# Gated linear attention into an activation-gated MLP: state decays taken by transfers through memory instead of by products on TensorE

## The chip, the cores and the metric

The kernel runs on one core of a Trainium2 chip. The metric is the device time of one execution in microseconds. TensorE (PE) multiplies matrices into PSUM, VectorE (DVE), ScalarE (ACT) and GpSimd (POOL) work elementwise, and SyncE (SP) issues most of the transfers between memory and the on-chip buffers. Each engine, and each issuing queue, takes its instructions in the order in which they stand in the program.

## What is computed

The first part is a recurrence per batch and head, over 768 steps with a head size of 48 (4 batches, 8 heads). The state is a 48 x 48 matrix; each of its rows decays by its own factor `alpha` at each step:

```python
for t in range(S):
    state = alpha[:, :, t, :, None] * state + np.einsum('bhd,bhe->bhde', k[:, :, t], v[:, :, t])
    y[:, :, t] = np.einsum('bhd,bhde->bhe', q[:, :, t], state)
```

The second part takes y as 3072 tokens of 384 numbers:

```python
h = x @ w_in            # 384 -> 2048
g = h * np.cos(h)
return (g @ w_out).astype(np.float32)   # 2048 -> 384
```

## The kernel before, in words

**Tiling.** The 768 steps of a batch are cut into 3 pairs of chunks; a pair has 256 steps, a chunk 128. With 4 batches there are 12 pairs, numbered J = 0 to 11. The pairs 0, 3, 6 and 9 begin a batch with an empty state. On chip, partition p of a pair holds the steps 2p and 2p + 1 (the index e), so that partitions 0 to 63 are the first chunk and 64 to 127 the second. The 8 heads are handled as 4 head pairs (`NP`), two heads of 48 numbers in 64 rows each.

**Decays.** Within a chunk the recurrence becomes matrix products, once q and k are scaled by the decay accumulated since the chunk began. `ln` takes the logarithm of alpha (for J >= 3 GpSimd first multiplies the two steps of a partition, `mul_a`, so that one sum is enough). `cums` adds the logarithms up with a triangular matrix on TensorE (lines 158 to 169). Its result has 384 columns, one per head and component, and a row per partition. Behind them, in 8 more columns, the same function puts four products (line 167), one per head pair: the logarithms' totals over each of the two chunks, but with the components lying along the partitions. `exps` takes the exponential of all this on ScalarE; for e = 1 it reads 392 columns (line 196).

**State.** The state of a head pair has its components along the partitions, so the factor by which a chunk makes it decay is wanted along the partitions too. `decay` (line 242) forms on GpSimd a small tile `c2_sb[J]` of 128 x (4 head pairs, 2 chunks, 2 heads) from the 8 columns, with zeros where row and head don't belong together (`dmask`). `outer` makes the products of k and v of a chunk, `add_state` adds the old state on VectorE, and `decay_state` (line 310) multiplies the sum by `c2_sb` on GpSimd, which gives the state that the next chunk's y reads.

**Other steps of a pair.** `scale_k` and `scale_q` (GpSimd or VectorE) multiply k and q by the exponentials; `trans` transposes them on TensorE; `scores` and `mask` give the part within a chunk; `castv` brings v to 16 bits on GpSimd; `stack_v` (line 221) restacks it by four SP transfers from on-chip to on-chip for J >= 3; `yT` makes y, transposed, from state, scores and stacked v. Then `mlp1`, the cosine, `gate` and `mlp2` run the second part, and `store` writes the result.

**Order.** A table written out by hand, `PLAN` (lines 433 to 498), has a row for each step and a column for each pair, with a planned time in nanoseconds; the steps are issued in the order of these times. The times set the order only. An instruction starts when its engine gets to it and its inputs are there. On SP stand the loads of alpha, k, q and v (48), the stacking transfers (36) and the stores. The pools give alpha 4 buffers and k, q and v 3 each.

```python
"load v": "3750 8250 35770 41770 51910 61570 67906 73970 75470 85710 95267 96757",
"eb": "- - - 43138 49360 59320 71283 83790 88947 103219 109067 127741",
"castv": "10660 16184 42680 48680 62906 71716 73380 94337 92617 104995 130491 144063",
"vst": "- - - 49610 63836 82270 79970 98527 102027 109974 131421 151922",
"trans": "14073 17773 40885 47348 58944 70064 80866 92234 109989 116249 127239 136001",
"state 0": "14460 23600 46802 51395 70936 89767 87087 104215 121237 120457 143283 156049",
"yT": "20503 26545 48000 58219 72693 91349 90719 109104 124433 140168 151138 162701",
```

The row `eb` is a pair's run of exponentials on ScalarE, the last of which (e = 1) has the values that the state's decay is made from.

Of the kernel before, what the change touches and what calls it, by code (L numbers as in the profile page):

```python
# [9 lines left out]
FP = mybir.dt.float32  # L10
# [6 lines left out]
def kernel(  # L17
# [10 lines left out]
    nc = tc.nc  # L28
    B, H, S, D = q.shape
    DM, DF = moe_w_in.shape  # L30
    C = 128
    HC = C // 2
    T2 = 2 * C
    NJB = S // T2
    NJ = B * NJB
    NP = H // 2
    HD = H * D
    KT = DM // C
    NF = DF // C
# [1 line left out]
    NU = NF // FW  # L41
    MP = 4

    NL, NQ, NV, NS = 4, 3, 3, 2
    BUF = {"a": 4, "in": 3, "cp": 3, "qkT": 3, "A": 2, "un": 4, "us": 2, "c": 3, "xT": 3, "g": 4}

    consts = ctx.enter_context(tc.tile_pool(name="consts", bufs=1))
    sb = ctx.enter_context(tc.tile_pool(name="sb", bufs=2))
    ps = ctx.enter_context(tc.tile_pool(name="ps", bufs=1, space=bass.MemoryType.PSUM))

    zeros = consts.tile([C, 512], BF, tag="zeros")
    nc.vector.memset(zeros, 0.0)  # L52
# [11 lines left out]
    for c in range(2):  # L64
        r = slice(HC * c, HC * c + HC)
# [14 lines left out]
    for lst, nm, n in ((lna_t, "lna", NL), (kh_t, "kh", NQ), (qh_t, "qh", NQ), (vp_t, "vp", NV)):  # L80
        for r in range(n):
            t = consts.tile([C, 2, H, 64], BF, tag=f"{nm}{r}", name=f"{nm}{r}")
            nc.vector.memset(t[:, :, :, D:64], 0.0)
            lst.append(t)
    for r in range(NS):
        t = consts.tile([C, 2, H, 64], BF, tag=f"vs{r}", name=f"vs{r}")
        nc.gpsimd.memset(t[:, :, :, D:64], 0.0)
        vs_t.append(t)
    dmask = consts.tile([C, 2], FP, tag="dmask")
    nc.vector.memset(dmask, 0.0)  # L90
    for a in range(2):
# [5 lines left out]
    a_sb, kqv, cp_sb, icp_sb, qkT_sb, A_sb, c2_sb = {}, {}, {}, {}, {}, {}, {}  # L97
# [36 lines left out]
    def act_set(which):  # L134
        if which == "exp" and act_now[0] != "exp":
            nc.scalar.preload_act_table_set("natural_log_exp_and_others")  # L136
        act_now[0] = which
# [14 lines left out]
    def sums(J, t, mats):  # L152
        o = t[:, 0:HD].rearrange("p (h d) -> p h d", h=H)
        for i, m in enumerate(mats):
            nc.tensor.matmul(o, m.rearrange("p c i -> p (c i)"), lna_t[J % NL][:, i, :, 0:D], start=(i == 0),
                             stop=(i == len(mats) - 1))

    def cums(J):
        if (J, 1) not in cums_ps:
            cums_ps[J, 1] = ps.tile([C, 512], FP, tag="x", name="cums", bufs=1)  # L160
        t = cums_ps[J, 1]
        lna = lna_t[J % NL]
        ne = 1 if J in both else 2
        sums(J, t, [tri, tri][:ne])
        for p in range(NP):
            for e in range(ne):
                nc.tensor.matmul(t[:, HD + 2 * p : HD + 2 * p + 2],
                                 lna[:, e, 2 * p : 2 * p + 2, :].rearrange("s h d -> s (h d)"), inchunk,
                                 start=(e == 0), stop=(e == ne - 1))
# [10 lines left out]
    def sub(J):  # L180
        cp_sb[J, 0] = sb.tile([C, HD], FP, tag="cp0", name="cp", bufs=BUF["cp"])
        nc.vector.tensor_tensor(out=cp_sb[J, 0].rearrange("p (h d) -> p h d", h=H),
                                in0=cums_ps[J, 1][:, 0:HD].rearrange("p (h d) -> p h d", h=H),
                                in1=lna_t[J % NL][:, 1, :, 0:D], op=ALU.subtract)

    def logs(J, e):
        return cums_ps[J, e] if (J, e) in cums_ps else cp_sb[J, e]

    def icp(J, e):
        act_set("exp")  # L190
        icp_sb[J, e] = sb.tile([C, HD], FP, tag=f"icp{e}", name="icp", bufs=BUF["cp"])
        nc.scalar.activation(out=icp_sb[J, e], in_=logs(J, e)[:, 0:HD], func=AF.Exp, scale=-1.0)  # L192

    def exps(J, e):
        act_set("exp")
        w = HD + 2 * NP * e
        t = logs(J, e)
        if (J, e) not in cp_sb:
            cp_sb[J, e] = sb.tile([C, w], FP, tag=f"cp{e}", name="cp", bufs=BUF["cp"])
        nc.scalar.activation(out=cp_sb[J, e], in_=t[:, 0:w], func=AF.Exp)  # L200

    def session(J):
        for e in range(2):
            icp(J, e)
        for e in range(2):
            exps(J, e)
        if J + 1 < NJ:
            ln(J + 1)
# [29 lines left out]
    def evict_vs(J, copy):  # L238
        copy(out=vs_t[J % NS][:, :, :, 0:D],
             in_=vs_ps.pop(J)[:, :, 0:HD].rearrange("s c (h d) -> s c h d", h=H))  # L240

    def decay(J):
        c2_sb[J] = sb.tile([C, NP, 2, 2], FP, tag="c2", name="c2", bufs=4)
        nc.gpsimd.tensor_tensor(
            out=c2_sb[J],
            in0=cp_sb[J, 1][:, HD : HD + 2 * NP].rearrange("r (p c) -> r p c", c=2).unsqueeze(3).to_broadcast([C, NP, 2, 2]),
            in1=dmask.unsqueeze(1).unsqueeze(1).to_broadcast([C, NP, 2, 2]),
            op=ALU.mult,
        )
# [3 lines left out]
    def trans(J):  # L253
        T_ps[J] = ps.tile([C, 2, 2 * NP, 2, HC], BF, tag="h", name="T_ps", bufs=3)
        for i, x in ((1, kh_t[J % NQ]), (0, qh_t[J % NQ])):
            for p in range(NP):
                for e in range(2):
                    for c in range(2):
                        r = slice(HC * c, HC * c + HC)
                        nc.tensor.transpose(T_ps[J][:, c, i * NP + p, e, :],  # L260
                                            x[r, e, 2 * p : 2 * p + 2, :].rearrange("s h d -> s (h d)"), ident_bf[r, r])

    def evict_T(J, c, copy):
        if J not in qkT_sb:
            qkT_sb[J] = sb.tile([C, 2, 2 * NP, C], BF, tag="qkT", name="qkT", bufs=BUF["qkT"])
        copy(out=qkT_sb[J][:, c], in_=T_ps[J][:, c].rearrange("r n e s -> r n (e s)"))  # L266
# [145 lines left out]
    def idle(n):  # L412
# [5 lines left out]
    copies = {"DVE": nc.vector.tensor_copy, "ACT": nc.scalar.copy}  # L418
    mults = {"DVE": nc.vector, "POOL": nc.gpsimd}
    steps = {  # L420
        "load": lambda J, nm: load(nm, J), "w1": load_w1, "w2": load_w2,
        "mula": mul_a, "ln": ln, "cums0": cums0, "cums": cums, "sub": sub, "icp": icp, "exps": exps, "eb": session,
        "sk": lambda J, e, eng="POOL": scale_k(J, e, mults[eng]), "sq": lambda J, e, eng="POOL": scale_q(J, e, mults[eng]),
        "castv": cast_v, "vst": stack_v, "vpe": stack_v_pe,
        "vev": lambda J, eng="DVE": evict_vs(J, copies[eng]), "decay": decay, "trans": trans,
        "evT": lambda J, c, eng="DVE": evict_T(J, c, copies[eng]), "scores": scores, "mask": mask, "outer": outer,
        "add": add_state, "state": decay_state, "yT": yT, "evy": lambda J, c, eng="ACT": evict_y(J, c, copies[eng]),
        "m1": mlp1, "sin": cosine, "gate": gate, "m2": mlp2, "evo": lambda J, c, eng="ACT": evict_o(J, c, copies[eng]),
# [73 lines left out]
    for key, line in PLAN.items():  # L502
        kind, *rest = key.split()
        for J, word in enumerate(line.split()):
            if word != "-":
                t, _, eng = word.partition(":")
# [38 lines left out]
```

## Time and profile before

| | us |
|---|---|
| median of 3 runs | 188.01 (187.84 to 188.37) |
| profiled execution | 188.32 |
| its span, first to last instruction | 186.5 |
| TensorE busy | 176.7 (95%) |
| VectorE busy | 135.4 (73%) |
| ScalarE busy | 126.5 (68%) |
| GpSimd busy | 77.1 (41%) |

A busy share is an average over the span. The weights and the first pairs fill the first 40 us or so; from then on pairs overlap, one in its attention part while earlier ones are in the MLP. Times in the profile's rows count from the start of the span. A row of a group or of the timeline gives its start, its length, the engine, the line of the kernel, what it writes and reads, and how often it occurs; in square brackets stands the idle time before it and what ended that. `SPq` is SP's issuing queue; the length of a row there is the time that the issue held the queue, not the transfer.

### The profile page before, as it was taken

The page shows a single profiled execution, that of the slowest core. Times are in us where ns is not written, and L with a number is a line of the kernel's source. Part 1 is how long each engine was busy: PE and PEld are TensorE (multiplying, and loading weights), DVE is VectorE, ACT ScalarE, POOL GpSimd, SP SyncE. Part 2 cuts the span into 40 slices and gives each one's busy share as a digit, 9 for nine tenths or more (in the row PEclk, how much of TensorE's full clock was granted, in tenths as well). Part 3 has the DMA queues.
Part 4 walks back from the last instruction along what each step waited for, and adds up shares of the span by engine and source line. Part 5 has one row for each costly group of instructions (what it writes and reads, how often), then busy time and mean ns, then how long its engine had stood idle before and what let it go on. Part 6 is the DMA issues. An engine that isn't in the chain of part 4 may idle for free.

```text
span 186.5 us, 5746 instructions
## 1 busy us (share of the span) xinstructions
PE 176.7 (95%) x2467; PEld 126.4 (68%) x2469; DVE 135.4 (73%) x184; ACT 126.5 (68%) x161; POOL 77.1 (41%) x110
## 2 busy tenths in 40 slices
PE   7988799989989999999999999999999999999993
PEld 2434588655667786785688668676867686786872
DVE  7178775589799979698847987794977556754461
ACT  2466876889498986889668999728965264373330
POOL 5079510257645653781896076930360320100000
PEclk9999999999999999999999999999999999999999
DMA  6999999999949979996799932600041005301102
GB/s 152 261 258 165 181 204 237 259 266 265 274 105 304 264 180 245 264 260 167 186 278 278 247 104 46 182 0 4 4 136 47 5 0 158 118 0 66 64 0 84
DMA packets 60137, 29.47 MB, mean 158 GB/s; under 512 B 51024, under 2 KB 60112, under 8 KB 60112
## 3 DMA queue, kind: packets, MB, share of 16 engines
q1 hardware_dynamic: 56256, 25.86, 57.2%
q0 software_dynamic: 3712, 3.15, 11.0%
q8 instruction: 19, 0.31, 0.7%
q10 hardware_dynamic: 144, 0.10, 0.2%
q14 instruction: 6, 0.05, 0.1%
HBM read 25.17 MB, written 4.72 MB: 160 GB/s over the span
## 4 chain that ended last, share of the span: by engine, by line
PE 73%; ACT 15%; DVE 8%; issue 3%; DVEq 0%
PE h_ps L361 31%; PE o_ps L390 24%; PE idle_ps L416 4%; PE y_ps L340 3%; ACT qkT L266 3%; DVE gsb L372 3%; PE T_ps L260 2%; ACT c_sb L367 2%; PE A_ps L274 2%; ACT L136 2%; ACT cp L200 2%; PE U_ps L291 2%; DVE kh L212 2%; ACT icp L192 2%; PE o_last L384 1%
## 5 line engine op out<-in xcount | busy, mean ns | idle before, releaser
L372 DVE TENSOR_TENSOR gsb<-h_ps,c_sb 128x1024 bf16<-128x1024 f32 x48 | 58.1, 1221 | 21.9 <-ACT c_sb L367 21.2
L367 ACT ACTIVATE c_sb<-h_ps,halfpi 128x1024 bf16<-128x1024 f32 x48 | 53.0, 1113 | 26.8 <-PE h_ps L361 23.0
L361 PE MATMUL h_ps<-xT,w 128*128 128x256 bf16 x576 | 66.7, 273 | 1.3 <-ACT xT L351 0.7
L390 PE MATMUL o_ps<-w,gsb 128*128 128x384 bf16 x368 | 66.7, 327 | 0.1
L361 PEld LDWEIGHTS <-w 128*128 128x128 bf16 x576 | 55.6, 98 | 10.1 <-issue 1.6
L390 PEld LDWEIGHTS <-gsb 128*128 128x128 bf16 x368 | 33.8, 98 | 21.2 <-DVE gsb L372 0.6
L313 POOL TENSOR_TENSOR un<-us,c 128x384 bf16<-128x384 f32 x20 | 16.7, 835 | 40.7 <-DVE us L305 29.1
L279 DVE TENSOR_TENSOR A_sb<-A_ps,msk 128x1024 bf16<-128x1024 f32 x24 | 28.9, 1215 | 1.7 <-PE A_ps L274 1.7
L212 POOL TENSOR_TENSOR kh<-k,icp 128x384 bf16<-128x384 f32 x17 | 16.9, 999 | 9.2 <-ACT icp L192 7.8
L216 POOL TENSOR_TENSOR qh<-q,cp 128x384 bf16<-128x384 f32 x15 | 15.0, 1006 | 11.8 <-ACT cp L200 11.8
L149 POOL TENSOR_TENSOR a<-a 128x384 f32<-128x384 f32 x9 | 9.0, 1001 | 12.6 <-DMA a<-in_alpha_dram 12.6
L219 POOL CAST vp<-v 128x768 bf16<-128x768 f32 x12 | 10.1, 841 | 8.8 <-DMA v<-in_v_dram 7.7
L416 PE MATMUL idle_ps<-zeros 128*128 128x512 bf16 x38 | 12.0, 457 | 1.4 <-DVE zeros L52 1.2
L141 ACT ACTIVATE lna<-a 128x768 bf16<-128x768 f32 x12 | 10.2, 847 | 4.6 <-DMA a<-in_alpha_dram 4.6
L266 ACT COPY qkT<-T_ps 128x1024 bf16<-128x1024 bf16 x8 | 8.0, 1015 | 6.9 <-PE T_ps L260 4.4
L136 ACT ACT_TABLE_LOAD x9 | 11.5, 1283 | 0.9 <-PEq L529 0.7
L367 ACT ACT_TABLE_LOAD x9 | 11.5, 1283 | 0.2
L266 DVE COPY qkT<-T_ps 128x1024 bf16<-128x1024 bf16 x16 | 10.8, 678 | 1.1 <-ACT qkT L266 1.1
L305 DVE TENSOR_TENSOR us<-U_ps,un 128x384 f32<-128x384 f32 x16 | 8.7, 550 | 3.8 <-PE U_ps L291 2.8
L402 DVE COPY o_sb<-o_ps 128x384 f32<-128x384 f32 x12 | 6.6, 551 | 6.5 <-PE o_ps L390 6.5
L351 ACT CAST xT<-y_ps 128x384 bf16<-128x384 f32 x12 | 6.7, 594 | 5.6 <-PE y_ps L340 3.8
L351 DVE CAST xT<-y_ps 128x384 bf16<-128x384 f32 x12 | 6.8, 584 | 4.7 <-PE y_ps L340 2.9
(69 smaller groups left out, 159.1 us busy)
## 6 DMA issues: line engine op xcount, KB each, us to landing
k<-in_k_dram SPq DMA_DIRECT2D x12, 384.0 KB, 6.0
a<-in_alpha_dram SPq DMA_DIRECT2D x12, 384.0 KB, 6.1
v<-in_v_dram SPq DMA_DIRECT2D x12, 384.0 KB, 6.0
q<-in_q_dram SPq DMA_DIRECT2D x12, 384.0 KB, 6.3
out_dram<-o_sb SPq DMA_DIRECT2D x23, 192.0 KB, 2.6
vs<-vp SPq DMA_DIRECT2D x36, 64.0 KB, 2.1
w<-in_moe_w_out_dram POOLq DMA_DIRECT2D x4, 384.0 KB, 10.1
w<-in_moe_w_in_dram POOLq DMA_DIRECT2D x4, 384.0 KB, 7.3
```

Source lines behind the costliest of these rows:

```text
L136: nc.scalar.preload_act_table_set("natural_log_exp_and_others")
L212: eng.tensor_tensor(out=kh_t[J % NQ][:, e, :, 0:D], in0=kqv["k", J][:, :, e], in1=icp_, op=ALU.mult)
L216: eng.tensor_tensor(out=qh_t[J % NQ][:, e, :, 0:D], in0=kqv["q", J][:, :, e], in1=cp, op=ALU.mult)
L266: copy(out=qkT_sb[J][:, c], in_=T_ps[J][:, c].rearrange("r n e s -> r n (e s)"))
L279: nc.vector.tensor_tensor(out=A_sb[J][:, c].rearrange("s a p t -> s (a p) t"), in0=A_ps.pop((J, c)).rearrange("s a p t -> s (a p) t"), in1 ...
L313: nc.gpsimd.tensor_tensor(out=u, in0=U_sum.pop(n), in1=c2_sb[J][:, :, c].unsqueeze(3).to_broadcast([C, NP, 2, D]), op=ALU.mult)
L351: copy(out=xT[J][:, :, c * C : (c + 1) * C].rearrange("r i (t e) -> r i e t", e=2), in_=y_ps[J][:, c, 0 : KT * C].rearrange("r (i e t) -> ...
L361: nc.tensor.matmul(h_ps[J, u][:, f, :], w1[:, kk, ft * C : (ft + 1) * C], xT[J][:, kk, :], start=(kk == 0), stop=(kk == KT - 1))
L367: nc.scalar.activation(out=c_sb[J, u], in_=h_ps[J, u], func=AF.Sin, bias=halfpi, scale=1.0)
L372: nc.vector.tensor_tensor(out=gsb[J][:, u * FW : (u + 1) * FW], in0=h_ps.pop((J, u)), in1=c_sb.pop((J, u)), op=ALU.mult)
L390: nc.tensor.matmul(o_ps[J, c][:, 0:DM], gsb[J][:, ft, c * C : (c + 1) * C], w2[:, ft], start=(ft == 0), stop=(ft == NF - 1))
L416: nc.tensor.matmul(idle_ps[0], zeros[:, 0:C], zeros, start=True, stop=True)
```

## The change

For the pairs 3 to 11 (`NE = 3`) the four products of `cums` are left out, and the exponential for e = 1 reads 384 columns instead of 392. The totals over a chunk are the last rows of the cumulative sums, so their exponentials stand already in the rows 63 and 127 of `cp_sb[J, 1]`. A new step `ends` writes these two rows (2 x 384 numbers of 4 bytes) to a scratch tile in memory, `[4, 2, 2, 48]`. `decay` then reads them back by two transfers, one for each head of the head pairs, into 48 partitions each, number by number, so that the components lie along the partitions. The target is one of four tiles `dec_t`, zeroed once by GpSimd at the start. All three transfers are issued by SP. GpSimd's multiply by `dmask` is gone for these pairs. The new step comes 2.3 us behind the planned start of the exponentials in `PLAN`, the reads 3.6 us behind `ends`.

```diff
+    NE = 3
...
-    NL, NQ, NV, NS = 4, 3, 3, 2
+    NL, NQ, NV, NS, ND = 4, 3, 3, 2, 4
...
+    dram = ctx.enter_context(tc.tile_pool(name="dram", bufs=1, space=bass.MemoryType.DRAM))
...
+    dec_t = []
+    for x in range(ND):
+        t = consts.tile([C, NP, 2, 2], FP, tag=f"dec{x}", name=f"dec{x}")
+        nc.gpsimd.memset(t, 0.0)
+        dec_t.append(t)
...
-        for p in range(NP):
+        for p in range(NP if J < NE else 0):
...
-        w = HD + 2 * NP * e
+        w = HD + (2 * NP * e if J < NE else 0)
...
+    ends_dram = {}
+
+    def ends(J):
+
+        ends_dram[J] = dram.tile([NP, 2, 2, D], FP, tag="ends", name="ends", bufs=3)
+        nc.sync.dma_start(out=ends_dram[J].rearrange("p c a d -> c p (a d)"),
+                          in_=cp_sb[J, 1][HC - 1 : C : HC, 0:HD].rearrange("c (p x) -> c p x", p=NP))
+
     def decay(J):
+        if J >= NE:
+            c2_sb[J] = dec_t[J % ND]
+            rows = ends_dram.pop(J)
+            for a in range(2):
+                nc.sync.dma_start(out=c2_sb[J][64 * a : 64 * a + D, :, :, a].rearrange("r p c -> r (p c)"),
+                                  in_=rows[:, :, a].rearrange("p c d -> d (p c)"))
+            return
...
-        "decay": "11579 11749 45180 49450 56180 80800 76050 92447 114345 115465 132991 146818",
+        "decay": "11579 11749 45180 49038 55260 65220 77183 89690 94847 109119 114967 133641",
+        "ends": "- - - 45438 51660 61620 73583 86090 91247 105519 111367 130041",
```

In the changed program SP's order around the places that the prediction names is: store, `ends` 3, load k 4, store, load q 4, the reads for pair 3, stacking of pair 3, `ends` 4, load v 4, load k 5, store, load a 7, the reads for pair 4, five loads (the last of them v 5), `ends` 5, stacking of pair 4, the reads for pair 5, store, load a 8, load v 6. TensorE's, VectorE's and ScalarE's other instructions keep their order.

More of the change, by code (lines that the diff above doesn't have):

```diff
@@ L424 @@
         "castv": cast_v, "vst": stack_v, "vpe": stack_v_pe,
-        "vev": lambda J, eng="DVE": evict_vs(J, copies[eng]), "decay": decay, "trans": trans,
+        "vev": lambda J, eng="DVE": evict_vs(J, copies[eng]), "ends": ends, "decay": decay, "trans": trans,
         "evT": lambda J, c, eng="DVE": evict_T(J, c, copies[eng]), "scores": scores, "mask": mask, "outer": outer,
```

## The prediction

> **What bounds the kernel now.** I read the page's busy shares first, then the windows by stage, then the timelines of TensorE, SP's queue and GpSimd around the places that the change touches. The page:
>
> ```profile
> span 186.5 us, 5746 instructions
> PE 176.7 (95%) x2467; PEld 126.4 (68%) x2469; DVE 135.4 (73%) x184; ACT 126.5 (68%) x161; POOL 77.1 (41%) x110
> PEclk9999999999999999999999999999999999999999
> q1 hardware_dynamic: 56256, 25.86, 57.2%
> out_dram<-o_sb SPq DMA_DIRECT2D x23, 192.0 KB, 2.6
> v<-in_v_dram SPq DMA_DIRECT2D x12, 384.0 KB, 6.0
> ```
>
> TensorE is busy nearly throughout, at full clock. GpSimd (POOL) has room. A load takes 6.0 us to land although a store on a quiet queue takes 1.9 (the shortest waits in SP's rows): SP's transfers stand in a line. The windows say where (columns: stretch, its length, then PE, PEld, DVE, ACT, POOL busy with counts, clock, DMA share, GB/s):
>
> ```profile
> 51.29:55.96 4.67, 4.08 (x56) 3.25 (x51) 4.54 (x7) 4.64 (x8) 2.24 (x3) 1.00 0.47 106
> 55.96:69.95 13.99, 13.97 (x187) 10.71 (x186) 12.69 (x16) 12.57 (x15) 8.03 (x10) 1.00 1.08 249
> 69.95:83.94 13.99, 13.73 (x237) 10.13 (x236) 11.38 (x15) 10.69 (x14) 9.29 (x12) 1.00 1.12 256
> 93.27:107.26 13.99, 13.87 (x251) 11.06 (x249) 10.31 (x12) 11.25 (x14) 7.80 (x10) 1.00 1.09 268
> 107.26:135.00 27.74, 27.44 (x439) 20.36 (x437) 22.01 (x29) 22.09 (x30) 14.54 (x18) 1.00 0.21 57
> ```
>
> From 56 to 84 us both TensorE and the DMA engines are full, so work added to SP's line comes out as later landings of everything behind it. After 107 us the DMA engines are a fifth busy. The change adds to the line in the first kind of stretch.
>
> **What it removes.** Nine pairs (the fourth to the twelfth) lose four products each on TensorE. One pair's cumulative sum and products:
>
> ```profile
> 54.48 0.33 PE L155 MATMUL cums<-lna,tri 128*128 128x384 bf16 x1
> 54.65 0.24 PE L167 MATMUL cums<-inchunk,lna 128*128 128x2 bf16 x4
> 54.76 1.49 PE L361 MATMUL h_ps<-xT,w 128*128 128x256 bf16 x12
> ```
>
> The record of 0.24 us is pipelined; from the first product's start to the next matmul's is 54.76 - 54.65 = 0.11 us. Nine times 0.11 is 1.0 us. The chain that ended last gives each group 0.08 us, so 0.7 us is the other bound; I take 0.9. GpSimd loses nine multiplies of 0.217 us (row of L244); it is off the path but for one place below. The exponential of the second half loses 8 of 392 columns: its 0.487 us against 0.471 for the same without them, 9 x 0.016 = 0.1 us on ScalarE, counted as nothing because ScalarE's idle time in front of it (1 to 4 us in most pairs) covers it. The four memsets of the new tiles (0.10 us each by the row of a small memset) fall into GpSimd's 7.3 us of idle time before its first cast.
>
> **What it adds to SP.** Per pair three issues: `ends` (8 pieces of 384 bytes to memory), then two reads of 384 pieces of 4 bytes each, 768 packets. Bounds of each price:
> - An issue: 0.33 us (shortest store) to 0.60 (the stacking transfers, 0.587 median). I take 0.5, as most of SP's issues here come close behind each other.
> - A 4-byte packet: 9 ns is the median of the 4-byte semaphore packets in the trace's packet records; the mean over the queue's packets is 57.2% x 186.5 x 16 / 56256 = 30 ns. No row has 4-byte data. Over 16 engines a pair's 48 packets per engine take 0.43 to 1.44 us; I take 0.45, since the records of 384, 1024 and 1536 bytes (25, 46 at the least, 62 ns) lie near a line that ends near 10 ns at no bytes.
> - `ends` to land: 1.9 us on a quiet queue, 6.1 at most for a store in the crowd; I take 4 to 5 where loads stand ahead of it.
>
> The Trainium skill, "DMA: Bandwidth & Descriptors", section "Rules for kernel authors", says that a last dimension that isn't contiguous is lowered to one descriptor per element; the count of 768 agrees with it, and no run here shows it yet. The same page's section "Bandwidth" gives about 10.5 ns per packet in its smallest transfer; an estimate by that is 48 x 10.5 = 0.50 us a pair, beside my 0.45.
>
> **Where it lands on the path.** SP issues in order, and the read of a pair waits until its own `ends` has landed; what stands behind waits too. SP's line before:
>
> ```profile
> 48.13 0.43 SPq L105 DMA_DIRECT2D q<-in_q_dram  x1
> 50.86 3.01 SPq L225 DMA_DIRECT2D vs<-vp  x4
> 62.92 2.38 SPq L105 DMA_DIRECT2D v<-in_v_dram  x1
> 65.93 3.50 SPq L225 DMA_DIRECT2D vs<-vp  x4
> 69.47 0.58 SPq L408 DMA_DIRECT2D out_dram<-o_sb  x1
> 70.10 0.46 SPq L105 DMA_DIRECT2D a<-in_alpha_dram  x1
> 70.61 0.68 SPq L105 DMA_DIRECT2D v<-in_v_dram  x1
> ```
>
> The last row is the v of pair 6 (pairs from 0). It landed at 75.61 us, and GpSimd, in order, was standing there for it:
>
> ```profile
> 75.76 0.83 POOL L219 CAST vp<-v 128x768 bf16<-128x768 f32 x1 [1.09 <-PE y_ps L340]
> 81.33 1.00 POOL L216 TENSOR_TENSOR qh<-q,cp 128x384 bf16<-128x384 f32 x1
> 83.34 0.41 PE L260 MATMUL T_ps<-ident_bf,kh 64*128 64x64 bf16 x16
> ```
>
> (The page names a matmul as releaser; the landing came 0.1 us before it.) From the cast to 83.45 GpSimd has no gap, and the product at 81.33 to 82.32 feeds the transposes at 83.34: a slack of 1.0 us, 1.2 once the multiply at 78.45 is gone.
>
> How late is that v? Ahead of it stand three pairs' nine new issues. Pair 3's fit into SP's gap of 2.3 us before 50.86, less its read's wait, and overshoot it; with `ends` of pair 4 that is 0.7 us at 56. Pair 4's reads are issued while loads hold SP back (1.4 to 2.4 us an issue), so that only their 0.45 us of packets count, and I let the ring's own stalls absorb that. Pair 5's `ends` goes out behind the v load of 62.92, which landed at 69.96, so it lands near 70.5, 1.0 us after the stacking transfers leave SP free; its two reads then cost 2 x 0.5 = 1.0 of issue and 0.4 of packets ahead of the v. Sum 0.7 + 1.0 + 1.0 + 0.4 = 3.1 us. TensorE stalls 3.1 - 1.2 = 1.9 us at the transposes. At the low prices (0.33, 9 ns, `ends` landed in time) the sum is 0.4 + 0 + 0.7 + 0.4 = 1.5, a stall of 0.3; at the high ones (0.60, 30 ns, 2.0 of wait) 0.9 + 2.0 + 1.2 + 1.4 = 5.5, a stall of 4.3.
>
> Other places. Pair 3's decay was used at 53.72; I put its landing at 53.4 to 54.2 (ends out at 46.5, landed near 50, reads out by 51, 2 to 3 us to land behind a k, a store and a q). VectorE's next use of that state came 1.0 us after it was ready, so 0.1 us counted, 0.7 at most. From pair 4 on the decay was used 10 us or more after it can land (73.07, 90.2, 92.9, 107.4). The stacked v of pairs 5 and 7 had 3.6 and 4.3 us before their y products at 94.4 and 112.4; the line will be 3 to 5 us late there, but TensorE itself is then 1.9 late, so nothing counted. After 107 us SP waits long for other things (11.4 us before 135.36), which hides pairs 9 to 11; stores that land late there cost nothing until a copy needs their buffer (0.95 us once before).
>
> Sum: -0.9 + 1.9 + 0.1 = +1.1 us. The profiled execution took 188.32 us (span 186.54), 0.31 above the median of 188.01; so 189.4 beside it, and 189.1 as a median.
>
> **Rivals.** A, faster: the line has more give than I count, because a load held back by a full ring absorbs SP's issues; then the v is under 1.2 us late and only the gain is left, 188.0 - 0.9 = 187.1. It decides at a lateness of 2.1 us (stall equal to gain). For it: SP's issue times of 1.4 to 2.4 us in 56 to 65 are waits, not work. Against: rows of 0.46 to 0.68 around the v, where SP was the limit. B, slower by much: a 4-byte packet costs 50 ns or more. Then a pair takes 2.4 us of every engine, the v of pair 6 is near 6 late (stall 4.6), and six pairs push the stacked v of pair 7 some 12 us, past its 4.3 and the stall: 188.0 + 4.6 + 3 = 195. Nothing in the rows speaks for 50 ns, but none shows a read of 4 bytes either. The Trainium skill, same page, "Specifications", says that transfers under 512 bytes are done as read and write-back; by that rule a packet would cost twice, 60 ns at the upper row, which is this rival. The 384-byte loads at 25 ns a packet show no such doubling. C: the two halves cancel, with a lateness between 1.5 and 2.7: 187.5 to 188.5.
>
> **Chances.** Mine (slower by 0.6 to 3 us) 0.43, A 0.25, B 0.19, C 0.13. Below 0.3% (0.56 us) this kernel's runs, 187.84 to 188.37, tell little from no change. Faster 0.26, same 0.14, slower 0.60. The likeliest case alone spans 188.6 to 191; the range takes in A's 187.1 and the lower part of B, 187.0 to 194.5.
>
> **What would show it.** Right: products of L167 fall from 60 to 24; SP's waits name the `ends` landing at the reads; GpSimd's cast of v of pair 6 stands about 3 us later, and TensorE is idle 1 to 3 us before that pair's transposes; GpSimd never waits long for a decay after pair 3. Wrong: no TensorE gap there (A), or DMA share above 1 well past 107 us and y products waiting for stacked v (B).

## The result and the profile after

The changed kernel takes 189.18 us (median; 188.80 to 189.62) where the kernel before, run beside it, takes 188.31 (187.84 to 188.40). The ratio is 1.0052 with an interval of 1.0034 to 1.0070: slower by 0.98 us by that ratio. The forecast was 1.1 us. The profiled execution that is read below took 189.34 us, span 187.6; the one of before 188.32, span 186.5. One execution further down, of the repeated change, showed a lower granted clock (0.989, 193.09 us) and is left out of every median and ratio.

The lines of the page of the changed kernel that answer to those of before:

```profile
span 187.6 us, 5704 instructions
PE 175.7 (94%) x2431; PEld 124.7 (66%) x2433; DVE 136.1 (73%) x184; ACT 126.7 (68%) x161; POOL 75.6 (40%) x105
...
q1 hardware_dynamic: 63546, 25.92, 59.2%
...
PE 58%; DMA 13%; ACT 9%; DVE 6%; SPq 5%; POOL 4%; issue 3%; POOLq 0%; ACTq 0%; DVEq 0%
```

TensorE has 36 matmuls less and is busy 1.0 us less, at the same clock, but its span is 1.1 us longer: it stands 2.1 us more. The last line shows where to look. It is the share of each engine in the chain that ended last; before the change it read 73% TensorE, 15% ScalarE, 8% VectorE and no transfer at all. Now 18% of the chain is transfers and SP's queue.

The reads themselves, by source line (duration of an issue in ns, least, median and most; then us from issue to landing in the same order):

```profile
L264 SPq DMA_DIRECT2D dec<-ends x18: 327/525/1137, 49.1 to 139.6; - x18
DMA to landing us min/median/max: 2.0/3.4/3.7
L256 SPq DMA_DIRECT2D ends<-cp x9: 539/553/1197, 46.8 to 133.7; - x9
```

They are cheap: half a us per issue. The view gives a landing for only four of the 18 reads, so 3.7 us is not the longest: pair 3's second read is issued at 50.15 us and lands at 54.44. And in the packet records of this trace the 7,200 or so packets that are new are 9 ns each (median of all that are 4 bytes long, 9,091 records). What they cost is order. This is the chain around pair 6's v (start, length, what):

```profile
66.06 3.69 DMA ends<-cp
69.76 0.97 SPq L264
...
72.28 4.95 DMA v<-in_v_dram
...
82.83 0.97 POOL qh L225
```

Pair 5's `ends` takes 3.69 us to land; SP waits for it at the head of the reads, 0.4 us beyond the stacking transfers; then the reads, a store and a load of alpha (`a`) go, and the v of pair 6 is issued at 72.28 instead of 70.61 and lands at 77.24 instead of 75.61. GpSimd casts it 1.6 us later, works without a gap up to the q product of pair 6, and TensorE's transposes of q wait for that. The changed kernel, and behind it the transposes of q before:

```profile
77.38 0.83 POOL L228 CAST vp<-v 128x768 bf16<-128x768 f32 x1 [2.62 <-DMA v<-in_v_dram]
...
83.30 0.41 PE L284 MATMUL T_ps<-ident_bf,kh 64*128 64x64 bf16 x16
83.85 0.41 PE L284 MATMUL T_ps<-ident_bf,qh 64*128 64x64 bf16 x16
```

```profile
83.58 0.40 PE L260 MATMUL T_ps<-ident_bf,qh 64*128 64x64 bf16 x16
```

Before, the second group of transposes followed the first (at 83.34) after 0.24 us, now after 0.55: a stall of 0.31 us, where the forecast had 1.9. It is in the right place and far too small. The rest comes from two places that the forecast had costed at nothing. The first is the y product of pair 7, whose stacked v landed 5.3 us later than before (113.46 against 108.12); the second is a store, which holds the buffer that ScalarE's next copy needs. After, and then the same product and copy before:

```profile
113.38 0.79 PE L364 MATMUL y_ps<-A_sb,vs 128*32 128x128 bf16 x32 [0.53 <-DMA vs<-vp]
...
142.24 0.48 ACT L426 COPY o_sb<-o_ps 128x384 f32<-128x384 f32 x1 [2.95 <-DMA out_dram<-o_sb]
142.77 2.11 PE L414 MATMUL o_ps<-w,gsb 128*128 128x384 bf16 x12 [0.47 <-ACT o_sb L426]
```

```profile
112.79 0.62 PE L340 MATMUL y_ps<-A_sb,vs 128*32 128x128 bf16 x32
140.03 0.48 ACT L402 COPY o_sb<-o_ps 128x384 f32<-128x384 f32 x1 [0.95 <-DMA out_dram<-o_sb]
```

The store stands behind the stacking of pair 10, which held SP 3.33 us instead of 2.39, and behind pair 11's reads, 1.07 us more. (Only the reads are known to be the change's doing; the longer hold occurs without any transfer too, as told below under late stores.) It goes out at 140.17 us instead of 137.85 and lands at 142.14 instead of 139.95. ScalarE waits 2.95 us for it (0.95 before), and TensorE's output matmuls wait for ScalarE.

How late TensorE is against before, from the starts of the same groups of matmuls in the two timelines (negative: ahead; gains of the left-out products are included):

| stretch, us | late by, us | what happened |
|---|---|---|
| to 60 | -0.06 | pair 3's reads, no stall |
| 63 to 67 | +0.34 | a product of VectorE took 1.16 us instead of 0.55; made good by 78 us |
| 83, before pair 6's transposes | -0.03 | |
| behind them | +0.28 | v of pair 6 |
| 106 to 112 | -0.13 | products left out |
| behind pair 7's y | +0.76 | stacked v of pair 7 |
| behind pair 9's transposes | +0.18 | a wait that was there before is gone |
| 131 to 141 | +0.21 | |
| 144.7 to the end | +1.26 | store |

So in this execution the last place decides: 1.05 of the 1.26 us come at the store.

### The profile page after: what moved, and what is told of

Read it like the earlier page. It is cut to its first block, busy times and chain, and to the rows that moved or that the text cites. A ratio compares the mean times of both kernels' runs of the same rounds, so it can differ in the third digit from the quotient of the medians.

```text
span 187.6 us, 5704 instructions
## 1 busy us (share of the span) xinstructions
PE 175.7 (94%) x2431; PEld 124.7 (66%) x2433; DVE 136.1 (73%) x184; ACT 126.7 (68%) x161; POOL 75.6 (40%) x105
## 3 DMA queue, kind: packets, MB, share of 16 engines
q1 hardware_dynamic: 63546, 25.92, 59.2%
## 4 chain that ended last, share of the span: by engine, by line
PE 58%; DMA 13%; ACT 9%; DVE 6%; SPq 5%; POOL 4%; issue 3%; POOLq 0%; ACTq 0%; DVEq 0%
PE h_ps L385 24%; PE o_ps L414 21%; DMA a<-in_alpha_dram 6%; PE y_ps L364 3%; ACT qkT L290 3%; DMA v<-in_v_dram 3%; DVE gsb L396 2%; ACT c_sb L391 2%; PE A_ps L298 2%; DMA ends<-cp 2%; PE T_ps L284 2%; PE U_ps L315 2%; SPq L234 2%; DMA vs<-vp 2%; DVE kh L221 2%
## 5 line engine op out<-in xcount | busy, mean ns | idle before, releaser
L337 POOL TENSOR_TENSOR un<-us,dec 128x384 bf16<-128x384 f32 x15 | 12.5, 835 | 40.3 <-DVE us L329 25.9
L440 PE MATMUL idle_ps<-zeros 128*128 128x512 bf16 x38 | 11.1, 428 | 1.4 <-DVE zeros L55 1.2
L426 ACT COPY o_sb<-o_ps 128x384 f32<-128x384 f32 x11 | 5.2, 477 | 8.2 <-PE o_ps L414 5.1
```

The lines of the kernel that those rows point to most:

```text
L337: nc.gpsimd.tensor_tensor(out=u, in0=U_sum.pop(n), in1=c2_sb[J][:, :, c].unsqueeze(3).to_broadcast([C, NP, 2, D]), op=ALU.mult)
L426: copy(out=t, in_=o_ps.pop((J, c))[:, 0:DM])
L440: nc.tensor.matmul(idle_ps[0], zeros[:, 0:C], zeros, start=True, stop=True)
```

## The experiments

The theory is that the price is lateness on SP's one queue: three issues a pair and the read's wait for its own `ends` push back loads, stackings and stores that have no slack. Its rivals: the left-out products themselves bring nothing or even cost; the number of small packets costs, wherever they stand; one single place (pair 3's late decay, pair 6's v, the store) makes the whole loss.

**The gain alone.** The products stay out, and nothing is transferred. This kernel leaves out the states that are carried from chunk to chunk in pairs 3 to 11, and serves for timing only.

```diff
         if J >= NE:
             c2_sb[J] = dec_t[J % ND]
-            rows = ends_dram.pop(J)
-            for a in range(2):
-                nc.sync.dma_start(...)
             return
...
-        "ends": "- - - 45438 51660 61620 73583 86090 91247 105519 111367 130041",
```

> The products are left out as in the change, but none of the transfers is made: the decays of pairs 3 to 11 are the zeros that the four tiles were filled with, so these states are left out of the result in effect. It measures the gain alone. Both theories: 36 products at 25 ns, of which the traces before and after show 0.8 us freed between matmuls: 0.6 to 0.9 us below the kernel before, ratio 0.995 to 0.997. If the gain is only there as long as nothing else limits, under 0.3 us.

Measured: 187.87 us against 188.40, ratio 0.9974 (0.9962 to 0.9986): a gain of 0.5 us (0.3 to 0.7), which lies between the two expectations. In its trace TensorE is ahead by 0.6 us from 110 us on.

**The cost alone.** Products and GpSimd's multiply stay for all pairs; the transfers are made and nobody reads the tiles.

```diff
-        for p in range(NP if J < NE else 0):
+        for p in range(NP):
...
+    def reads(J):
+        rows = ends_dram.pop(J)
+        for a in range(2):
+            nc.sync.dma_start(out=dec_t[J % ND][64 * a : 64 * a + D, :, :, a]..., in_=rows[:, :, a]...)
...
+        "reads": "- - - 49038 55260 65220 77183 89690 94847 109119 114967 133641",
```

> All products and GpSimd's multiplies stay as before; the 27 transfers are made as in the change, to tiles that nothing reads. It measures the cost alone. If gain and cost simply add, the cost is what the change lost plus the gain: 0.9 + 0.8 = 1.7 us above the kernel before (1.3 to 2.1). If waiting for the decay itself costs (a state that stands for its transfer), this is well under 1.3, because nothing waits for these tiles.

Measured: 189.71 us, ratio 1.0071 (1.0044 to 1.0098): a cost of 1.3 us (0.8 to 1.8). Cost and gain add up to 0.8, which fits the change's 0.98 within the intervals. The products do bring something, so the first rival is out; the loss lies in the transfers. In this kernel's profile pair 6's transposes are held 1.0 us and pair 7's y 0.9 us.

**Half of the pairs each.** The change for the pairs 3 to 8 alone, and for 9 to 11 alone; the others keep the products and the decay of before.

```diff
-    NE = 3
+    NE, N2 = 3, 9      # or 9, 12
...
-        if J >= NE:
+        if NE <= J < N2:
```

> The change for pairs 3 to 8 only; pairs 9 to 11 as before. Theory V (as predicted): the loss comes from the crowded stretch of 46 to 107 us, through v of pair 6 and the stacked v of pair 7; then this kernel is 0.7 us or more above the kernel before, all of the change's loss or more. Theory S: the loss that lasts is made at 140 us, where ScalarE's copy stands for a store that pair 11's transfers delayed; then this kernel is within 0.5 us of the kernel before, and TensorE is 0 to 0.3 us late at 140 us.

> The change for pairs 9 to 11 only. Theory V: nothing is crowded there, the three pairs' gain of 0.25 us is left: 0 to 0.3 below the kernel before. Theory S: ScalarE waits 2 us or more for a store near 140 us and the kernel is 0.5 to 1.0 us above the kernel before.

Measured: pairs 3 to 8 188.98 us, ratio 1.0031 (1.0008 to 1.0054), +0.6 us; pairs 9 to 11 188.63 us, ratio 1.0016 (0.9996 to 1.0035), +0.3 us with an interval that takes in nothing. Together +0.9, the change's own loss. Each value lies between what the two theories had named. By the medians neither half makes it all, though the first half's interval (0.2 to 1.0 us) reaches the change's 0.98, so this pair of runs alone doesn't settle it. The profile of the second half has a hold of TensorE of 0.90 us at 99.3 us, ahead of every changed pair and named by nothing that the profile shows, and the store's wait of 2.1 us then costs only 0.17; so it does not settle what the store is worth.

The profile of the first half shows the one thing that the forecast had as a bound: pair 3's reads landed at 56.23 us, and GpSimd, VectorE and TensorE stood in a row behind them (its timeline):

```profile
56.38 0.83 POOL L337 TENSOR_TENSOR un<-us,dec 128x384 bf16<-128x384 f32 x1 [5.71 <-DMA dec<-ends]
57.25 0.56 DVE L329 TENSOR_TENSOR us<-U_ps,un 128x384 f32<-128x384 f32 x1 [1.78 <-POOL un L337]
57.87 2.36 PE L385 MATMUL h_ps<-xT,w 128*128 128x256 bf16 x20 [1.78 <-DVE us L329]
```

In the changed kernel's profile, whose program is the same up to there, these reads landed at 54.44 and TensorE did not stand there. So pair 3 has next to no slack, and a landing that varies by 1.8 us decides whether it costs.

**Pair 3 left as before, and then the same transfers put elsewhere.** The first kernel has the change for the pairs 4 to 11 only. The second issues just as many transfers of the same kind, but pair 5's and pair 8's stand behind the loads and stackings that they were ahead of, and pair 11's reads behind the stores:

```diff
-    NE = 3
+    NE, N2 = 4, 12
...
-        "decay": "11579 11749 45180 49450 55260 65220 77183 89690 94847 109119 114967 133641",
-        "ends": "- - - - 51660 61620 73583 86090 91247 105519 111367 130041",
+        "decay": "11579 11749 45180 49450 55260 76000 77183 89690 105000 109119 114967 137000",
+        "ends": "- - - - 51660 68000 73583 86090 102500 105519 111367 130041",
```

> The change for pairs 4 to 11; pair 3 keeps its products. In the profiles pair 3's reads landed at 54.4 in one execution and at 56.2 in another, where VectorE can wait until about 54.7. If that is a cause of the loss, the times lie closer together than the change's and the median comes 0.1 to 0.8 us below it (one pair's gain of 0.1 us is given up, and three issues ahead of v of pair 6 are gone). If it is not, the same as the change or 0.1 above.

> Pair 3 keeps its products; the transfers of pair 5 stand behind v of pair 6, those of pair 8 behind the stacking transfers of pair 8, the reads of pair 11 behind three stores. Only the place of transfers on SP's queue changes. If the loss is made of the four places (pair 3's late decay, v of pair 6, the stacked v of pair 7, the store at 140 us), all four are eased and the gain is what is left: 0.2 to 0.5 us below the kernel before, 187.9 to 188.2. If the transfers cost in another way (contention for the engines, longer issues everywhere), it stays at 188.8 or more.

Measured on one chip: 190.79 us, ratio 1.0136 (1.0100 to 1.0173), and 188.09 us, ratio 0.9994 (0.9973 to 1.0016). The same 24 transfers, with the same packets, cost 2.7 us more or less by their place in the queue. The first kernel misses what was expected of it: without pair 3 it is, on this chip, no closer to the kernel before. This takes out the number of packets as a cause, and pair 3 as the only one. The kernel with the early places, its waits (engine and line, what it waited for, us in total, times, longest) and pair 6's transposes in its timeline:

```profile
ACT o_sb L426 <- DMA out_dram<-o_sb: 3.0, 1, 3.0
PE T_ps L284 <- POOL qh L225: 1.2, 1, 1.2
PE y_ps L364 <- DMA vs<-vp: 1.1, 1, 1.1
```

```profile
83.23 0.41 PE L284 MATMUL T_ps<-ident_bf,kh 64*128 64x64 bf16 x16
84.82 0.41 PE L284 MATMUL T_ps<-ident_bf,qh 64*128 64x64 bf16 x16 [1.18 <-POOL qh L225]
```

The kernel with the late places, its timeline there:

```profile
83.03 0.41 PE L284 MATMUL T_ps<-ident_bf,kh 64*128 64x64 bf16 x16
83.57 0.41 PE L284 MATMUL T_ps<-ident_bf,qh 64*128 64x64 bf16 x16
```

From k's transposes to q's it is 1.59 us in the first and 0.54 in the second (0.24 before the change). Pair 7's y still waits 0.8 us and ScalarE 2.1 us for a store in the second; its profiled execution is its longest, 189.60 us, 1.5 above its median, so the median need not have these waits.

**Single places.** On that same chip only pair 11's reads were put behind the stores, and, in another kernel, the stores got six buffers instead of four:

```diff
-        "decay": "... 114967 133641",
+        "decay": "... 114967 137000",
```

```diff
-            t = sb.tile([C, DM], FP, tag="o_sb", name="o_sb", bufs=4)
+            t = sb.tile([C, DM], FP, tag="o_sb", name="o_sb", bufs=6)
```

> The change, with one row moved: the two reads of pair 11 stand behind the three stores that they stood ahead of. If the store that lands late at 140 us is one of the causes, ScalarE's wait for a store near 140 us falls from 2.95 us to 2 or less, and the kernel comes 0.2 to 1.0 us below the change: 188.2 to 189.0. If all the lasting loss is made before 110 us, no difference to the change.

> The change with 6 buffers for the stored rows instead of 4, so that the copy need not wait for a store. If the wait for a store is a cause: the same 0.2 to 1.0 us below the change or somewhat more, and no wait of ScalarE for a store. If not: the same as the change, 189.2.

Measured: 190.18 us, ratio 1.0091 (1.0067 to 1.0116), and 189.20 us, ratio 1.0050 (1.0026 to 1.0074). The first lies above the 188.2 to 189.0 that was expected of a cause, the second at the 189.2 that was to mean none, but neither can be ranked against the change, which was not run on that chip. What their profiles show: with six buffers no copy waits for a store, and the loss is not gone; with the reads put later ScalarE still waits 2.1 us for the store (2 or less was expected), since the stacking of pair 10 ahead of it begins 1.9 us later than before the change and holds SP 3.5 us. In both, pair 6's transposes are held (0.9 and 1.2 us). So the store is a place of its own but not the whole.

**The change again, and with one load moved.** The unaltered change, and the change with nothing but the v load of pair 6 issued ahead of the stacking of pair 4 and of pair 5's reads:

```diff
-        "load v": "3750 8250 35770 41770 51910 61570 67906 73970 75470 85710 95267 96757",
+        "load v": "3750 8250 35770 41770 51910 61570 63000 73970 75470 85710 95267 96757",
```

> The change itself, unaltered, beside the next three on the same chip. Its profile before showed TensorE only 0.3 us held up at pair 6's transposes, where the kernels with one row moved showed 0.9 to 1.25. If the size of that stall differs from execution to execution, the time is again 188.8 to 190.2 and the profile shows v of pair 6 landing between 77 and 79. If the moved rows themselves made it worse, 189.2 and a stall of 0.3 again.

> The change, with one load moved: v of pair 6 is issued ahead of pair 4's stacking transfers instead of behind them, two stores' and loads' places earlier. Nothing is taken away. Theory V (the late v of pair 6 is the largest cause): it lands before 75 us, GpSimd's cast doesn't wait for it, TensorE goes through pair 6's transposes without a gap, and the kernel is 0.3 to 1.3 us below the change on this chip. If the stall there is made good later anyway, less than 0.2.

Measured: 190.56 us, ratio 1.0104 (1.0080 to 1.0128), and 190.17 us, ratio 1.0074 (1.0052 to 1.0095). So the change costs 2.0 us on this chip (1.5 to 2.4) where it cost 1.0 on the first, more than was expected of it. The moved load is worth 0.4 us by the medians and 0.6 by the ratios, but the two intervals overlap, so that a gain is likely and not shown. Its profile shows this place mended and no other: the v lands at 73.9 us and the transposes follow each other, while ScalarE still waits 3.3 us for a store and pair 7's y 0.8 us for its stacked v.

**All places mended, and its control.** The later places of the transfers from above, pair 3 as before, v of pair 6 earlier, three of the last loads (v 10, q 11, v 11) later so that pair 7's stacking goes ahead of them, and six store buffers; and the kernel before with the same three loads, the same v 6 and the same buffers, without the change.

```diff
-        "load q": "5250 6750 29125 38770 48970 56370 57870 60070 78470 84570 87104 96187",
-        "load v": "3750 8250 35770 41770 51910 61570 67906 73970 75470 85710 95267 96757",
+        "load q": "5250 6750 29125 38770 48970 56370 57870 60070 78470 84570 87104 108000",
+        "load v": "3750 8250 35770 41770 51910 61570 63000 73970 75470 85710 106000 113000",
```

> The transfers as in the run with transfers later (pair 3 keeps its products), and besides: v of pair 6 earlier, three loads that are needed 28 us or more after they land (v of pair 10, q and v of pair 11) behind the stacking transfers of pair 8, and 6 buffers for stored rows. If lateness on SP's line is the whole cost, all four places are clear and the gain of the left-out products shows: 187.6 to 188.0, 0.4 to 0.8 us below the kernel before. If it stays at the kernel before's time or above, something of the transfers' cost is not lateness.

> The kernel before with the same moves of loads and the same 6 buffers, no transfers: the control for the run above. The kernel before has nothing to make good at these places except 0.3 us at pair 9's transposes and 0.1 of a late store, so it should stay within 0.3 us of the kernel before; the difference between this and the run above is then what leaving out the products brings, 0.4 to 0.7 us.

Measured on the chip of the change's repetition: 188.09 us, ratio 0.9970 (0.9951 to 0.9988), and 188.50 us, ratio 1.0004 (0.9985 to 1.0023). The first is 0.6 us faster than the kernel before (0.2 to 0.9) and 2.5 faster than the change beside it; the moves alone bring nothing. The difference of the two, 0.34% or 0.6 us (0.1 to 1.1, an estimate from both intervals), fits the gain of the left-out products, 0.5 in the kernel without transfers. The transfers of eight pairs are still there; no cost of theirs is left that these intervals would show. Its transposes and pair 7's y, without a gap:

```profile
83.52 0.41 PE L284 MATMUL T_ps<-ident_bf,kh 64*128 64x64 bf16 x16
83.77 0.40 PE L284 MATMUL T_ps<-ident_bf,qh 64*128 64x64 bf16 x16
...
112.28 0.52 PE L364 MATMUL y_ps<-qkT,un 128*32 128x128 bf16 x24
112.62 0.68 PE L364 MATMUL y_ps<-A_sb,vs 128*32 128x128 bf16 x32
```

## Why the prediction was right, and where it was not

The time, its sign and the mechanism were right: work on SP's queue made transfers late that had too little slack, and this outweighed the products. The split of the sum was partly wrong, and that the sum came within 0.1 us is luck.

- *The gain, 0.9 us.* Too high. Alone it is 0.5 (0.3 to 0.7). The forecast took some 0.1 us for each of nine pairs. In the trace of the kernel without transfers the way from a pair's sum to the next matmul shrinks by 0.08 to 0.10 us for six pairs and by nothing for pairs 4, 5 and 6: 0.55 us together. Pair 5 is the one whose rows the forecast shows: the next matmul starts 0.28 us behind the sum with the products and without them. What holds it there is not shown.
- *The prices.* Right or near: 0.525 and 0.553 us an issue (0.5 taken), 9 ns a packet (9), 3.7 us for pair 5's `ends` (4 to 5). The queue's share grew from 57.2% of 186.5 us to 59.2% of 187.6, which is 4.4 us for nine pairs, 0.49 a pair against 0.45. Rival B needed 50 ns and is out. (The shortest record of 1024 bytes is 44 ns in the trace, where the forecast has 46; its line changes by nothing that matters.) The Trainium skill, "DMA: Bandwidth & Descriptors", section "Specifications", has transfers under 512 bytes done as read and write-back; the doubling that the rival took from it does not show at 9 ns.
- *Pair 6's v, the 1.9 us.* The failed term. The chain goes over exactly the steps that the forecast named, but the v was 1.6 us late instead of 3.1 in the changed kernel's profile, near the low end of the bounds, and the stall was 0.31. The seven earlier issues of the change had left nothing behind when SP was done with pair 4's stacking, at 69.32 us against 69.43 before: the issue of pair 5's v held SP 1.56 us instead of 2.38 and the stacking 2.61 instead of 3.50. This is the give that rival A described, real but not enough. What was left is the wait for pair 5's `ends`, 0.4 us instead of 1.0, and its two reads, 1.5 us where the forecast had 1.0 and 0.4. The slack was a little larger too: the forecast measured its 1.2 us to the transposes of k, but the late product feeds those of q, 0.24 us behind. In the profiles of other kernels with the same early transfers the v landed at 78.0 to 79.0 us, 2.4 to 3.4 late, with stalls of 0.4 to 1.35 in the same measure.
- *"Nothing counted" for the stacked v of pairs 5 and 7.* Wrong for pair 7. The forecast set its lateness of 3 to 5 us against a slack of 4.3 and the stall of TensorE ahead of it; it was 5.3 late, and TensorE had no stall to cover it. (The product that reads the stacked v started at 112.79, not 112.44, so the slack was 4.7; 5.3 less 4.7 is 0.6, and the row has 0.53 of idle time.) It cost 0.9 us there in the profile, of which 0.6 came back at pair 9's transposes; 0.4 to 1.4 in the others.
- *Late stores "cost nothing until a copy needs their buffer".* The condition came true at 140 us: 1.05 us in this profile, the largest single item, 0.2 to 1.4 in others. Two things delay this store, and only the first is known to be the change's doing: pair 11's reads ahead of it, and one issue of pair 10's stacking that took 1.47 us instead of 0.59. The kernel without any transfer has such an issue there as well (1.34 us), so the transfers are not needed for it. The reads alone, behind a stacking of 2.43 or 2.44 us, cost TensorE 0.16 and 0.17 us (the cost alone, the pairs 9 to 11). A long stacking without the reads ahead of the store cost 0.2 or nothing. Both together cost 1.05 to 1.4.
- *Pair 3's decay, 0.1 us, 0.7 at most.* It landed at 54.44 us, just beyond the 54.2 of the forecast, and cost nothing in this profile; in another kernel's, where it landed at 56.23, TensorE stood 1.8 us, beyond the bound. It is no needed part of the loss, since the kernel without it lost as well.

- *The signs.* TensorE has the 36 products less, SP waits for `ends` at the reads, and GpSimd waits for a decay at pair 3 alone (3.8 us). The cast of pair 6's v stood 1.6 us later where about 3 was named, and the gap at the transposes was 0.3 us, not 1 to 3. Of rival B's two signs one came as well, a y product that waits for its stacked v; the other did not, as the DMA share from 107.26 to 135.00 us is 0.44 (0.21 before) and not above 1.

So the total fits because one stall that was too large stood for three smaller ones and for a gain that was too large. What stays open is why the change costs 1.0 us on one chip and 2.0 on another with the kernel before at 188.3 and 188.5. The v landings above, 77.2 to 79.0 us, and the one long issue are of the right size for it: several places at the edge of their slack turn small differences of landing times into stalls. But this is argued, not shown.

## What to carry to other kernels

On this kernel's in-order queue a tiny transfer cost what it made late behind it, not its bytes, and a read that waited for its own write held everything behind it. So list the loads, stackings and stores behind each new transfer with the slack of their consumers, all of them down to the end of the stretch, and put the new pair behind those that have none: here the same 24 transfers took 190.8 or 188.1 us by place alone. Only then does a saving of half a microsecond on the bounding engine show.

## What the runs showed of the hardware

- Transfers of single 4-byte elements were cheap: 9 ns a packet, and a read of 384 such elements landed in 2.0 us at best, beside 1.9 us for a store on a quiet queue (3.4 is the median of the four reads whose landing the view gives).
- An issue held SP's queue 0.33 us when nothing was outstanding and 1.4 to 2.4 us while several loads were outstanding. A queue held in this way gave back the time of issues ahead of it: after seven new ones SP was done with pair 4's stacking at 69.32 us, against 69.43 before.
- Pair 10's stacking held SP 2.39 to 2.44 us in four of the profiles and 3.0 to 3.7 in the others, by one long issue each. In each of the others one 16 KB packet of the queue that the page calls `q8 instruction` falls into the stacking (at 136.64 us in the changed kernel); in the four it comes earlier (132.39 before the change). That the packet is the cause, and what places it, is not shown.
- VectorE's product of q took 1.16 us with GpSimd's own product running beside it, and 0.55 us in the kernel before, where GpSimd's was over:

```profile
58.26 1.00 POOL L225 TENSOR_TENSOR qh<-q,cp 128x384 bf16<-128x384 f32 x1
58.51 1.16 DVE L225 TENSOR_TENSOR qh<-q,cp 128x384 bf16<-128x384 f32 x1
```

GpSimd's product ends at 59.26; VectorE's, if it could do nothing until then, would end 0.55 us later, at 59.81, and it ends at 59.67. A second pair of products, in the kernel before, agrees: GpSimd's product of k ends at 67.82, and VectorE's of q, started at 67.44, ends at 68.23 where this reckoning gives 68.37. The Trainium skill, "SBUF — State Buffer", section "SBUF: two separate sides", says that the two engines share a pair of ports, that a VectorE operation with two inputs in SBUF and a GpSimd operation lock it for the whole instruction, and that the later one is fully blocked. The trace agrees to 0.14 us. Here GpSimd's product stood 0.88 us later than before the change (58.26 against 57.38), and that doubled a product of VectorE.
